# Preparing q, k and v of a block-sorted attention in front of an FFN: batch 0 on 128 partitions and five PSUM banks, v of batches 1 to 3 sorted as the moving operand and scattered through HBM

## The chip, the cores and the metric

One core of a Trainium2 chip runs the whole kernel. The metric is the device time of one execution in microseconds. Unless said otherwise, times inside the execution are counted from the first instruction of the profiled execution (the "span").

## The reference

Inputs: q, k and v of shape (4, 8, 768, 64), `sort_net` (4, 8, 8, 8), FFN weights (512 x 2048 and 2048 x 512) and `alpha` (2048), all fp32. Output: (3072, 512) fp32.

```python
P = sort_net
for _ in range(5):
    P = exp(P - max(P, -1)); P /= sum(P, -1); P /= sum(P, -2)     # eps 1e-9 in each sum
k_sorted = einsum('bhij,bhjcd->bhicd', P, k in 8 blocks of 96)     # the same for v
scores = q_block @ k_sorted_block.T / 8                            # block by block
attn_out = softmax(scores) @ v_sorted_block
x = attn_out.transpose(0, 2, 1, 3).reshape(3072, 512)
h = x @ w_in
out = (max(h, 0) + alpha * min(h, 0)) @ w_out
```

So each (batch, block) pair is an independent attention over 96 rows for 8 heads. There are 32 such pairs; the text calls them groups 0 to 31, eight to a batch.

## The kernel before

**How the order is made.** The kernel adds operations to a graph (`G.add`: engine, function, planned duration, read and write keys, priority). `schedule` (L87) orders them on each engine by planned times and priorities; `emit` (L169) writes five in-order instruction streams with semaphore waits. On the chip nothing is reordered: an instruction that waits holds everything behind it on its engine. DMAs are issued by POOL (loads that cast fp32 to bf16, and so use its software queue) and SP (the small loads, transposes, outputs). `fill` (L152) puts dummy matmuls (L743) into planned gaps of PE up to a time limit.

**Sinkhorn** (L403). P lies as 32 x 64 on DVE; each of five rounds is exponential (ACT, L413), row sum, reciprocal, product, column sum, reciprocal, product (DVE, L415 to L424); round 1 adds eps to the column sums (L421). `spread_k` and `spread_v` (L427, L442) turn P into block matrices BDK and BDV by a small matmul and three DVE operations.

**K of a batch** (`prep_k`, L480): 6 units, each 16 matmuls of 64x64 and one copy of 512 columns from PSUM into KT. **V of a batch**: 8 reshaping copies (`conv_v`, L498, from VST with c and d exchanged into VD), then 8 units (`prep_v`, L510) of 8 matmuls with a slice of VD as the stationary operand and BDV as the moving one, and a copy of each into VS[n]. VS has for each head and block 64 columns and a column of ones, which gives the softmax sums. For batch 0, VST holds 64 partitions; batches 2 and 3 share one set of 8 copies. **Q**: batch 0 by 24 transposing matmuls and 12 copies (`prep_q`, L458) into QTz, in which the other head's 64 rows are zero (two DVE memsets, L373); batches 1 to 3 by loads into QN (zeroed by a POOL memset, L376) and six DMA transposes each on SP (`turn_q`, L345). The next loads of QN wait for the transposes of the batch before.

**Attention of a group** (L531): scores (L544), maxima on DVE (L549), scores again with the maxima subtracted (L557, L562), exponential on ACT (L568), product with VS (the "PV", L576), division by the sums (L581, L584), transposition (L593), copy to xT. **FFN** (L605, L633): FFN1 in chunks of 2, 2 and then 4 groups, 16 row tiles each, through two banks of psH: four matmuls (L613), a Relu on ACT (L621), a DVE operation (L624) into hT. FFN2 is 16 matmuls of 512 columns per 128 tokens (L645), a copy, an output DMA.

**Order of the issue.** POOL: q, k, v of batch 0, w_in in four parts, w_out in two, the memset of QN, k, v and q of batch 1, and the rest as buffers come free. Batch b + 1 is prepared among the groups of batch b. PSUM: psS, psO, psH two banks each, psY and psP one each; the preparation of batch 0 goes through psP and psH.

Of the kernel before, what the change touches and what calls it, by code (L numbers as in the profile page):

```python
# [13 lines left out]
NB = 8  # L14
# [8 lines left out]
XR = 1536  # L23
EPS = 1e-9
# [31 lines left out]
class _Graph:  # L56
# [30 lines left out]
    def schedule(self):  # L87
# [30 lines left out]
        while done < len(ops):  # L118
# [14 lines left out]
            if op.dma is not None:  # L133
                free[e] = at + (600 if e == "pool" else 100)
                begin = max(dma_free if e == "pool" else 0, free[e] + 700)
                if e == "pool":
                    dma_free = begin + dur
                op.end = begin + dur + (1500 if e == "pool" else 500)
            else:
                op.end = free[e] = at + dur  # L140
# [11 lines left out]
    def fill(self, make, unit, first, before):  # L152

        out, last = [], self.ops[first].end + 300
        for op in self.order["pe"]:
            n = int((op.start - last) * 0.9 / unit)
            if op.start < before and n > 0:
# [79 lines left out]
def bass_sinkhorn_attn__then__act_prelu_kernel(  # L237
# [38 lines left out]
    selv = sb("selv", [32, 2, 128], F32)  # L276
# [3 lines left out]
    BDV = sb("BDV", [128, 2, 128], BF16)  # L280
# [4 lines left out]
    xT = sb("xT", [128, KT_TILES, XR], BF16)  # L285
    hT = sb("hT", [128, FT_TILES, RING], BF16)
# [6 lines left out]
    KT = [sb("KT%d" % n, [128, 4, S], BF16) for n in range(2)]  # L293
    VS = [sb("VS%d" % n, [96, 64, 65], BF16) for n in range(2)]
    nm = [sb("nm%d" % n, [96, 8], BF16) for n in range(2)]
    Esb = [sb("Esb%d" % n, [96, 8, 96], BF16) for n in range(2)]
# [8 lines left out]
    psY = ps("psY", [128, 512], F32)  # L305
    psP = ps("psP", [128, 512], F32)
    psPb = psP.bitcast(BF16)
    psOb = psO.bitcast(BF16)
    psHb = psH.bitcast(BF16)
    BANK_P = (psP, psPb, 0, 512, PSP)  # L310
    BANK_H = [(psH, psHb, x * 512, 1024, [("psH", x, 0), ("psH", x, 1)]) for x in range(2)]
# [22 lines left out]
    def load_q(b, prio):  # L334
# [4 lines left out]
        for h in range(H):  # L339
# [3 lines left out]
                load_us / 8, r=["QN0"], w=[("QN", h)], prio=prio, dma=(d_qn[h], 0))  # L343

    def turn_q(b, t, prio):  # L345
# [5 lines left out]
            w=[("QTz", n, u, x, y) for u in range(3) for x in range(2) for y in range(2)] if t == 0 else [("QTzt", n, t)],  # L351
# [6 lines left out]
    def load_v(b, prio):  # L358
        G.add(POOL, lambda e: e.dma_start(
# [5 lines left out]
    def consts():  # L365
# [6 lines left out]
        for hp in range(2):  # L372
            G.add(DVE, lambda e, hp=hp: e.memset(  # L373
                AP(QTz[0], (1 - hp) * 64 * 6144 + hp * 3072, [[6144, 64], [1, 3072]]), 0.0),
                850, w=[("QTz0", 0, hp)], prio=-89)
        G.add(POOL, lambda e: e.memset(QN[:, :, :, :], 0.0), 6000, w=["QN0"], prio=-20)  # L376
        for n in range(2):
            G.add(DVE, lambda e, n=n: e.memset(AP(VS[n], 64, [[64 * 65, 96], [65, 64]]), 1.0), 200,
                  w=[("VS1", n)], prio=-60 + 30 * n)

        def red(o, src, w):
# [6 lines left out]
              r=["identf"], w=["mkj"], prio=-70)  # L388
        red(mvh[:, :], AP(identf, 0, [[128, 128], [8, 16], [1, 8]]), "mvh")
        red(mvj[:, :], AP(identf, 0, [[128, 128], [1, 8], [8, 16]]), "mvj")  # L390
        for t, w, name in ((selk, 16, "selk"), (selv, 8, "selv")):
            G.add(ACT, lambda e, t=t, w=w: copy(e, AP(t, 0, [[32 * w, 32], [w, 32], [1, w]]),
                                                AP(identf, 0, [[128, 32], [1, 32], [0, w]])), 600,
                  r=["identf"], w=[name], prio=-66)
        return ib.idx
# [7 lines left out]
    def sinkhorn():  # L403
# [4 lines left out]
        for it in range(5):  # L408
# [11 lines left out]
            if it == 0:  # L420
                dv(lambda e: e.tensor_scalar(out=cs[:, :], in0=cs[:, :], scalar1=EPS, scalar2=None,  # L421
                                             op0=AluOpType.add), ["cs"], ["cs"])
# [4 lines left out]
    def spread_k(b, prio):  # L427
        G.add(PE, lambda e: e.matmul(psP[:, 0:64], AP(selk, b * 128, [[512, 32], [1, 128]]),
                                     P32[:, :]), 500, r=["P", "selk"], w=PSP, prio=prio)
        G.add(DVE, lambda e: e.tensor_tensor(  # L430
            out=AP(dtmp, 0, [[64, 128], [8, 8], [1, 8]]), in0=AP(psP, 0, [[512, 128], [8, 8], [1, 8]]),
# [10 lines left out]
    def spread_v(hf, prio):  # L442
        G.add(PE, lambda e: e.matmul(psP[:, 0:64], AP(selv, hf * 128, [[256, 32], [1, 128]]), P32[:, :]),
              500, r=["P", "selv"], w=PSP, prio=prio)
        G.add(DVE, lambda e: e.tensor_tensor(
            out=AP(dtmp, 0, [[64, 128], [8, 8], [1, 8]]), in0=AP(psP, 0, [[512, 128], [8, 8], [1, 8]]),
# [5 lines left out]
            out=AP(BDV, hf * 128, [[256, 128], [8, 16], [1, 8]]),  # L452
            in0=AP(mvh, 0, [[16, 128], [1, 16], [0, 8]]),
            in1=AP(dsel, 0, [[8, 128], [0, 16], [1, 8]]), op=AluOpType.mult), 290,
            r=["dsel", "mvh"], w=[("BDV", hf)], prio=prio)


    def prep_q(b, u, prio, bank=BANK_P):  # L458
        n = b % 2
        _, t, off, row, keys = bank  # L460

        def f(e):
            inst = None
            for p in range(8):
                pr = 8 * u + p
                inst = e.matmul(AP(t, 2 * off + p * 128, [[2 * row, 128], [1, 128]]),
                                AP(QS[n], pr * 128, [[3072, 128], [1, 128]]),
                                identb[:, :], is_transpose=True)
            return inst
        G.add(PE, f, t_pe(*[(128, 128)] * 8), r=[("QS", n), "identb"], w=keys, prio=prio)  # L470
        for cp in range(2):
            for hp in range(2):
                o = AP(QTz[n], hp * 64 * 6144 + hp * 3072 + cp + 16 * u,
# [24 lines left out]
    def conv_v(b, u, prio):  # L498
        hf = b // 2
        row, rows, keys = (0, 128, (0, 1)) if b == 2 else ((b % 2) * 64, 64, (b % 2,))  # L500
        if b == 3:
            return
# [161 lines left out]
    for u in range(3):  # L664
        prep_q(0, u, -50, ([BANK_P] + BANK_H)[u])
# [120 lines left out]
```

## Time and profile before

| what | value |
|---|---|
| time, median of 3 runs | 297.44 us (293.62 to 298.7) |
| the profiled execution | 295.86 us, its span 293.9 us |
| mean granted PE clock over the span | 0.936 |
| PE busy | 271.6 us (92%), 2827 matmuls |
| PE weight loads busy | 191.9 us (65%) |
| DVE busy | 189.5 us (64%) |
| ACT busy | 155.2 us (53%) |
| POOL busy | 35.3 us (12%) |
| HBM read / written | 27.28 MB / 6.29 MB |

The busy shares are means over unlike stages. PE's busy time is modelled from pipelined matmuls: it counts a matmul running at half clock, or one with gaps inside its pipeline, as busy too. "Granted clock" is the share of its full rate that the TensorE clock had. In the lines of the timeline, the columns are start, duration, engine, line, operation, output and inputs; a count "x8" merges eight in a row, and brackets give idle time before it and what ended it.

### The profile page before, as it was taken

What the parts mean: (1) busy time and instruction counts of PE and PEld (TensorE: products, weight loads), DVE (VectorE), ACT (ScalarE), POOL (GpSimd) and SP (SyncE); (2) the same over time, 40 slices, a digit from 0 to 9 for tenths busy, and PEclk for the clock granted to TensorE, in tenths of its full rate; (3) what the DMA queues carried; (4) which work ended last, traced back from release to release, by engine and by line L of the source; (5) the groups of instructions that cost most, each with busy time, mean ns of one, the idle gap of its engine ahead of it and who ended that gap; (6) DMA issues with size and microseconds to landing.
All of it is one profiled execution on the core that took longest, in us unless ns stands there. A gap on an engine that the chain in (4) does not pass through costs nothing.

```text
span 293.9 us, 6514 instructions
## 1 busy us (share of the span) xinstructions
PE 271.6 (92%) x2827; PEld 191.9 (65%) x2862; DVE 189.5 (64%) x360; ACT 155.2 (53%) x274; POOL 35.3 (12%) x45
## 2 busy tenths in 40 slices
PE   5909999995997999999999999999999999999995
PEld 5907898883885577776666666766666666655542
DVE  7978356796686578967566766666666666654510
ACT  3079622389689455664545544674454444444421
POOL 8980100001800620000000000000000000000000
PEclk9965555799999999999999999999999999999999
DMA  6999999982999990001671101000101000100111
GB/s 114 214 201 193 213 202 189 182 149 49 195 117 165 148 84 3 4 34 38 153 99 38 38 1 38 36 36 2 38 36 39 36 2 36 38 36 36 38 71 71
DMA packets 46619, 25.07 MB, mean 85 GB/s; under 512 B 38512, under 2 KB 42624, under 8 KB 46336
## 3 DMA queue, kind: packets, MB, share of 16 engines
q0 software_dynamic: 24048, 13.63, 33.6%
q1 hardware_dynamic: 22544, 11.03, 15.4%
q8 instruction: 22, 0.36, 0.5%
q14 instruction: 5, 0.04, 0.0%
HBM read 27.28 MB, written 6.29 MB: 114 GB/s over the span
## 4 chain that ended last, share of the span: by engine, by line
PE 81%; ACT 9%; DVE 7%; issue 2%
PE psH L613 26%; PE psY L645 23%; PE psS L544 4%; PE psS L562 4%; PE psS L557 4%; ACT VD L314 4%; PE psO L576 4%; PE psP L519 4%; PE psS L645 4%; DVE cs L421 2%; PE psY L743 2%; PE psO L593 2%; PE psP L489 2%; ACT t L621 1%; ACT Esb L568 1%
## 5 line engine op out<-in xcount | busy, mean ns | idle before, releaser
L624 DVE SCALAR_TENSOR_TENSOR hT<-t,omaT,psH 128x384 bf16<-128x384 f32 (+1 forms) x144 | 80.2, 566 | 56.5 <-ACT t L621 55.7
L613 PE MATMUL psH<-xT,w_in_bf 128*128 128x384 bf16 (+1 forms) x576 | 101.6, 310 | 4.1 <-DVE hT L624 4.1
L621 ACT ACTIVATE t<-psH 128x384 f32<-128x384 f32 (+1 forms) x144 | 64.2, 454 | 64.2 <-PE psH L613 63.7
L645 PE MATMUL psY<-w_out_bf,hT 128*128 128x512 bf16 x302 | 78.6, 379 | 2.1 <-issue 0.2
L613 PEld LDWEIGHTS psH<-xT,w_in_bf 128*128 128x128 bf16 x576 | 50.3, 99 | 27.8 <-DVE hT L624 5.5
L645 PEld LDWEIGHTS psY<-w_out_bf,hT 128*128 128x128 bf16 x336 | 31.1, 98 | 27.2 <-ACT outstg L314 0.4
L568 ACT ACTIVATE Esb<-psS 96x768 bf16<-96x768 f32 x32 | 25.9, 808 | 27.1 <-PE psS L562 26.6
L549 DVE TENSOR_REDUCE nm<-psS 96x8 bf16<-96x768 f32 x32 | 30.4, 951 | 8.4 <-PE psS L544 7.0
L557 PE MATMUL psS<-QTz,KT 128*96 128x192 bf16 x128 | 27.0, 263 | 0.0
L562 PE MATMUL psS<-identb,nm 96*96 96x96 bf16 x256 | 27.0, 216 | 0.0
L562 PEld LDWEIGHTS psS<-identb,nm 96*96 96x96 bf16 x256 | 25.7, 133 | 1.8
L584 DVE TENSOR_TENSOR xq<-psO,rec 96x512 bf16<-96x512 f32 x32 | 22.0, 686 | 1.1
L340 POOL DMA_DIRECT2D QN<-in_q_dram x24 | 19.9, 885 | 18.7 <-DMA QTz<-QN 18.5
L743 PE MATMUL psY<-identb 128*128 128x128 bf16 x201 | 18.3, 263 | 3.3 <-ACT identb L314 3.3
L314 ACT ACTIVATE VD<-VST 64x768 bf16<-64x768 bf16 (+1 forms) x14 | 21.2, 1525 | 0.1
L576 PEld LDWEIGHTS psO<-VS,Esb 96*96 96x96 bf16 x256 | 16.8, 131 | 5.1 <-ACT Esb L568 0.9
L544 PEld LDWEIGHTS psS<-KT,QTz 128*96 128x96 bf16 x256 | 16.5, 133 | 4.1 <-ACT Esb L568 0.5
L557 PEld LDWEIGHTS psS<-QTz,KT 128*96 128x96 bf16 x128 | 16.9, 132 | 2.8
L544 PE MATMUL psS<-KT,QTz 128*96 128x96 bf16 x256 | 18.3, 218 | 0.4 <-ACT Esb L568 0.4
L743 PEld LDWEIGHTS psY<-identb 128*128 128x128 bf16 x201 | 15.5, 119 | 4.1 <-ACT identb L314 3.3
L576 PE MATMUL psO<-VS,Esb 96*96 96x65 bf16 x256 | 17.4, 214 | 0.3 <-ACT Esb L568 0.2
L314 ACT ACTIVATE outstg<-psY 128x512 f32<-128x512 f32 x21 | 12.6, 599 | 8.2 <-PE psY L645 8.2
(77 smaller groups left out, 220.6 us busy)
## 6 DMA issues: line engine op xcount, KB each, us to landing
out_dram<-outstg SPq DMA_DIRECT2D x24, 256.0 KB, 2.0
KS<-in_k_dram POOLq DMA_DIRECT2D x4, 768.0 KB, 16.6
VST<-in_v_dram POOLq DMA_DIRECT2D x4, 768.0 KB, 19.8
QN<-in_q_dram POOLq DMA_DIRECT2D x24, 96.0 KB, 9.1
w_in_bf<-in_moe_w_in_dram POOLq DMA_DIRECT2D x4, 512.0 KB, 18.9
w_out_bf<-in_moe_w_out_dram POOLq DMA_DIRECT2D x2, 1024.0 KB, 28.3
QS<-in_q_dram POOLq DMA_DIRECT2D x1, 768.0 KB, 7.0
QTz<-QN SPq DMA_TRANSPOSE x18, 3.4
```

The source lines that it names most:

```text
L314: return e.activation(o, i, ACTF.Copy) if e is nc.scalar else e.tensor_copy(o, i)
L544: inst = e.matmul(AP(psS, (s // 4) * 512 + (s % 4) * 96, [[1024, 96], [1, 96]]), AP(QTz[n], hp * 3072 + h4 * 768 + i * 96, [[6144, 128], [ ...
L549: G.add(DVE, lambda e: e.tensor_reduce(AP(nm[m], 0, [[8, 96], [4, 2], [1, 4]]), AP(psS, 0, [[1024, 96], [512, 2], [96, 4], [1, 96]]), Axis ...
L557: e.matmul(AP(psS, base, [[1024, 96], [1, 192]]), AP(KT[n], h4 * 768 + i * 96, [[3072, 128], [1, 96]]), AP(QTz[n], h4 * 768 + i * 96, [[61 ...
L562: inst = e.matmul(AP(psS, base + hp * 96, [[1024, 96], [1, 96]]), AP(nm[m], 2 * h4 + hp, [[8, 96], [0, 96]]), AP(identb, 0, [[128, 96], [1 ...
L568: G.add(ACT, lambda e: e.activation(AP(Esb[m], 0, [[768, 96], [384, 2], [1, 384]]), AP(psS, 0, [[1024, 96], [512, 2], [1, 384]]), ACTF.Exp ...
L576: inst = e.matmul(AP(psO, hp * 512 + h4 * 68, [[1024, 96], [1, 65]]), AP(Esb[m], s * 96, [[768, 96], [1, 96]]), AP(VS[n], ((hp * 4 + h4) * ...
L613: inst = e.matmul(AP(psH, hb * 512, [[1024, 128], [1, n]]), AP(w_in_bf, kt * DFF + ft * 128, [[KT_TILES * DFF, 128], [1, 128]]), AP(xT, kt ...
L621: G.add(ACT, lambda e: e.activation(AP(t1[tb], 0, [[384, 128], [1, n]]), AP(psH, hb * 512, [[1024, 128], [1, n]]), ACTF.Relu, scale=-1.0), ...
L624: G.add(DVE, lambda e: e.scalar_tensor_tensor(out=AP(hT, ft * RING + tok % RING, [[FT_TILES * RING, 128], [1, n]]), in0=AP(t1[tb], 0, [[38 ...
L645: inst = e.matmul(AP(bank[0], bank[1], [[row, 128], [1, 512]]), AP(hT, ft * RING + tok % RING, [[FT_TILES * RING, 128], [1, 128]]), AP(w_o ...
L743: inst = e.matmul(psY[:, 0:128], identb[:, :], identb[:, :])
```

## The change

In words:

- L421's addition of a constant becomes an addition of two tensors, with a small tile of eps. The two memsets of QTz go. POOL's memset of QN is cut into eight, which fill only the halves that no load writes. A new POOL memset zeroes 16 pad columns of VD.
- Batch 0: v is loaded onto 128 partitions (two halves of each block), first of the three; q is loaded last. `conv_v` is four copies; `prep_v` 8 units of 16 matmuls of 64x64; the 96 rows of a block stand as 48 + 16 (zero) + 48 in the 112 rows of VS[0]. K gets 16 columns of padding by a copy (`KTpad`). The column of ones becomes a DVE copy from a tile `one0`, which is 0 in the pad rows. `prep_q` works like `prep_k` with the identity, without zero rows; scores of batch 0 are matmuls over 64 rows of one head. The 20 units of k, v and q go through five banks. Groups 0 and 1 use different banks for scores and outputs.
- Batches 1 to 3: v is sorted by matmuls with BDV as the stationary operand and VST as the moving one (512 columns, 12 per batch; batches 2 and 3 in the same 12 steps), copied to VD, written to an HBM tensor, and read back into VS in pieces of 64 elements. Each batch has two halves; all these DMAs go through SP's queue.
- The spreads of batches 1 to 3 are bound behind group 1. The planner's constants for POOL's DMAs (1500 to 2500 ns) and the dummy matmuls' limits change.

The core of the diff:

```diff
-        for hp in range(2):
-            G.add(DVE, lambda e, hp=hp: e.memset(
-                AP(QTz[0], (1 - hp) * 64 * 6144 + hp * 3072, [[6144, 64], [1, 3072]]), 0.0),
-                850, w=[("QTz0", 0, hp)], prio=-89)
-        G.add(POOL, lambda e: e.memset(QN[:, :, :, :], 0.0), 6000, w=["QN0"], prio=-20)
+        G.add(DVE, lambda e: e.memset(epst[:, :], EPS), 100, w=["eps"], prio=-89)
+        G.add(POOL, lambda e: e.memset(AP(VD, 48, [[6144, 128], [64, 64], [1, 16]]), 0.0), 900,
+              w=["VD0"], prio=-95.5)
+        for h in range(H):
+            G.add(POOL, lambda e, h=h: e.memset(
+                AP(QN, h * 128 + (1 - h // 4) * 64, [[6144, 128], [1024, 6], [1, 64]]), 0.0),
+                400, w=[("QN0", h)], prio=-21)
...
+        G.add(DVE, lambda e: e.tensor_copy(AP(VS[0], 64, [[64 * 65, 112], [65, 64]]), AP(one0, 0, [[1, 112], [0, 64]])),
+              200, r=["one0"], w=[("VS1", 0)], prio=-70)
...
-                dv(lambda e: e.tensor_scalar(out=cs[:, :], in0=cs[:, :], scalar1=EPS, scalar2=None,
-                                             op0=AluOpType.add), ["cs"], ["cs"])
+                dv(lambda e: e.tensor_tensor(out=cs[:, :], in0=cs[:, :], in1=epst[:, :], op=AluOpType.add),
+                   ["cs", "eps"], ["cs"])
...
     def load_v(b, prio):
+        if b == 0:
+            G.add(POOL, lambda e: e.dma_start(
+                AP(VST, 0, [[6144, 128], [1, 3072]]),
+                AP(v.tensor, 0, [[3072, 2], [6144, 64], [1, 3072]])),
+                load_us, w=[("VST", 0), ("VST", 1)], prio=prio, dma=(d_v[0], 0))
+            return
...
+    def prep_q(u, prio, bank):
+        t, off, row, keys = bank
+        G.add(PE, pairs(QS[0], 0, u, identb, 0, 128, bank), 8 * 33, r=[("QS", 0), "identb"], w=keys, prio=prio)
+        o = AP(QTz[0], 8 * u, [[6144, 128], [96, 32], [48, 2], [1, 8]])
+        i = AP(t, off, [[row, 128], [2, 32], [1, 2], [64, 8]])
+        G.add(EITHER, lambda e: copy(e, o, i), t_either(512), r=keys, w=[("Q0", u)], prio=prio)
...
+        if b == 0 and u == 1:
+            G.add(DVE, lambda e: e.tensor_copy(AP(KT[0], 48, [[ld, 128], [bk, 32], [1, 16]]),
+                                               AP(KT[0], 0, [[ld, 128], [bk, 32], [1, 16]])), 500,
+                  r=[("KT", 0, 0), ("KT", 0, 1)], w=["KTpad"], prio=prio + 1)
+
+    def conv_v(u, prio):
+        o = AP(VD, 16 * u * 64, [[6144, 128], [64, 16], [1, 48]])
+        i = AP(VST, 16 * u, [[6144, 128], [1, 16], [64, 48]])
+        G.add(EITHER if u == 3 else ACT, lambda e: copy(e, o, i), {"act": 1520, "dve": 890},
+              r=[("VST", 0), ("VST", 1)] + ["P"] * (u == 3), w=[("VD", u)], prio=prio)
...
+    def sort_v(bs, c, prio):
+        row, rows, keys = (bs[0] % 2) * 64, 64 * len(bs), [("VST", b % 2) for b in bs]
+
+        def f(e):
+            inst = None
+            for b in bs:
+                r0 = (b % 2) * 64
+                inst = e.matmul(AP(psYP, r0 * 1024 + 512, [[1024, 64], [1, 512]]),
+                                AP(BDV, r0 * 384 + (b // 2) * 128 + r0, [[384, 64], [1, 64]]),
+                                AP(VST, r0 * 6144 + c * 512, [[6144, 64], [1, 512]]))
+            return inst
+        G.add(PE, f, 300, r=keys + [("BDV", b // 2) for b in bs], w=PSP, prio=prio)
+        G.add(EITHER, lambda e: copy(e, AP(VD, row * 6144 + c * 512, [[6144, rows], [1, 512]]),
+                                     AP(psYP, row * 1024 + 512, [[1024, rows], [1, 512]])), t_either(512), r=PSP,
+              w=[("VN", c, b % 2) for b in bs] + ([("VD", u) for u in range(4)] + ["VD0"] if c == 0 else []), prio=prio)
+
+    def turn_v(b, x, prio):
+        r0, n = (b % 2) * 64, b % 2
+        G.add(SYNC, lambda e: e.dma_start(AP(scr, b * 64 * 6144 + x * 3072, [[6144, 64], [1, 3072]]),
+                                          AP(VD, r0 * 6144 + x * 3072, [[6144, 64], [1, 3072]])),
+              4000, r=[("VN", c, b % 2) for c in range(6 * x, 6 * x + 6)], w=[("scr", b, x)], prio=prio,
+              dma=(d_vo[2 * b + x], 0))
...
+        G.add(SYNC, lambda e: e.dma_start(AP(VS[n], x * 48 * 64 * 65, [[64 * 65, 48], [65, 64], [1, 64]]),
+                                          AP(scr, b * 64 * 6144 + x * 3072, [[64, 48], [6144, 64], [1, 64]])),
+              9000, r=[("scr", b, x), ("VS1", n)],
+              w=[("VS", n)] + [("VSu", u) for u in range(8)] * (n == 0) if x == 0 else [("VSx", n)],
+              prio=prio, dma=(d_vi[2 * b + x], 0))
...
-    load_q(0, -98)
+    load_v(0, -98)
     load_k(0, -97)
-    load_v(0, -96)
+    load_q(0, -96)
...
+    for u in range(4):
+        conv_v(u, -50)
+    bank = 0
+    spread_k(0, -48)
+    spread_v(2, -47.5)
+    for name, count, prio in (("k", 6, -47), ("v", 8, -45), ("q", 6, -46)):
+        for u in range(count):
+            x = BANKS0[bank % 5]
+            bank += 1
+            prep_k(0, u, prio, x) if name == "k" else prep_v(u, prio, x) if name == "v" else prep_q(u, prio, x)
...
-            units = ([(prep_k, u) for u in range(6)]
-                     + [(conv_v, u) for u in range(8)] + [(prep_v, u) for u in range(8)])
+            vs = ([1],) if b == 0 else ([2, 3],) if b == 1 else ()
+            if b == 2 and i == 0:
+                for x in range(2):
+                    turn_v(3, x, 8 * b - 7)
+            units = ([(f, x, c) for x in vs for y in range(2) for f, c in
+                      [(sort_v, c) for c in range(6 * y, 6 * y + 6)] + [(None, y)]]
+                     + [(prep_k, b + 1, u) for u in range(6)])
```

## The prediction

> **What bounds the kernel now.** I read the stage table first (the busy time of each engine in chosen stretches), then the timeline of the start, then the waits of PE, then the DMA queues. Columns of the stage table: stretch, its length, busy us and count of PE, PEld, DVE, ACT, POOL, granted clock, DMA share, GB/s.
>
> ```profile
> 0.00:24.00 24.00, 13.33 (x182) 13.04 (x183) 19.86 (x47) 10.69 (x19) 19.89 (x25) 0.87 0.99 179
> 24.00:50.00 26.00, 25.77 (x296) 22.59 (x295) 14.89 (x33) 13.02 (x16) 1.10 (x2) 0.50 1.40 196
> 50.00:74.00 24.00, 19.91 (x283) 16.09 (x285) 18.12 (x38) 17.11 (x30) 1.99 (x4) 0.89 0.77 135
> 74.00:98.00 24.00, 21.50 (x291) 17.11 (x294) 17.20 (x36) 19.38 (x35) 5.73 (x7) 1.00 1.19 165
> 98.00:146.00 48.00, 47.61 (x543) 33.83 (x549) 35.35 (x61) 26.84 (x50) 6.56 (x8) 1.00 0.40 57
> ```
>
> From 98 us on PE has no gap: only less PE work or an earlier start can move the end. Before 98 us PE is late or half idle, and from 24 to 50 us it runs at clock 0.50. The timeline says why the start is late:
>
> ```profile
> 6.12 7.32 DVE L421 TENSOR_SCALAR cs<-cs 32x8 f32<-32x8 f32 x1
> 8.13 5.29 POOL L376 MEMSET QN<- 128x6144 bf16 x1
> 13.71 0.26 DVE L424 TENSOR_TENSOR P<-P,cs 32x64 f32<-32x64 f32 x1
> 21.98 0.69 PE L428 MATMUL psP<-P,selk 32*128 32x64 f32 x2 [7.32 <-DVE P L424]
> 52.61 1.47 PE L613 MATMUL psH<-xT,w_in_bf 128*128 128x192 bf16 x8
> 95.04 0.51 PE L576 MATMUL psO<-VS,Esb 96*96 96x65 bf16 x8
> ```
>
> An addition to 256 numbers takes 7.32 us and ends at 13.44, as POOL's memset ends (13.42): DVE was held by POOL. P is ready at 21.9, the first FFN matmul runs at 52.6, and the ninth PV product (L576, group 8, the first of batch 1) at 95.0. From there to the end are 293.9 - 95.0 = 198.9 us, nearly all PE work. Last, the DMA side, which the change will load:
>
> ```profile
> 50.20 13.64 SPq L347 DMA_TRANSPOSE QTz<-QN  x6
> 75.02 0.38 SPq L655 DMA_DIRECT2D out_dram<-outstg  x1
> 87.73 8.61 SPq L347 DMA_TRANSPOSE QTz<-QN  x6
> ```
> ```profile
> 98.25 6.56 POOL L340 DMA_DIRECT2D QN<-in_q_dram  x8 [18.52 <-DMA QTz<-QN]
> ```
> ```profile
> DMA packets 6367, 1.35 MB, mean 168 GB/s; under 512 B 6288, under 2 KB 6288, under 8 KB 6355
> ```
>
> The first fence is SP's queue: batch 1's transposes start when q has landed, at 50.2, and hold SP for 13.6 us; batch 2's hold it for 8.6. The second is POOL: a batch of q takes 6.6 us to issue, and only after the transposes of the batch before. The third is the DMA page of 42 to 50 us, when batch 1's q arrives: 6288 small packets in 8 us, 786 per us. Until then the queue carries weights and inputs at some 200 GB/s, and the change alters neither their bytes nor, but for the order inside them, their place: q of batch 1 still lands near 50.2.
>
> **The change, part by part.** The sum is made on the profiled execution (span 293.9, time 295.86, so 2 us lie around the span); it is 1.6 us below the median of 297.44.
>
> Sinkhorn. L421 becomes a two-operand addition; its neighbour L417 takes 0.21, so -7.1. The two memsets of QTz (1.34 each) go, and the first exponential can start after selk (3.8) instead of 4.84: -1.0. P would be ready at 13.8. But the new ones column of VS (line 402 of the changed kernel, a DVE copy from SBUF to SBUF) stands between rounds 1 and 2 of the chain, at about 6 us, when POOL is again busy: issues till about 9 (before: 8.1, plus about 0.9 for the new memset of VD, 1024 elements at 0.86 ns), then eight memsets of QN, half the elements in all. It may cost nothing, or hold DVE until POOL's memsets end near 13, as L421 was. I take a release between two of the eight memsets, near 9.5: P at 9.5 + 4 rounds of 1.87 = 17; ends 13.8 and 21.
>
> The rule that speaks against this step is in the Trainium skill, "SBUF — State Buffer", Who interferes with whom: a DVE copy in a two-port mode and a GpSimd instruction exclude each other for the whole instruction, and the later one waits. L421 (7.32 us) agrees. By the rule alone, with POOL's eight memsets taken as one occupation, the copy would wait to about 13 and P come at 21; with the copy free, at 13.8; the end would be the same, as the sum below shows.
>
> Preparation of batch 0. Q no longer goes through 12 copies of 0.75 on ACT/DVE but through 6 units like K; V keeps 8 units, its 8 reshaping copies (1.5 on ACT, 0.9 on DVE) become 4. 20 units follow BDK (P + 2.5, as now 21.9 to 24.3): on PE each is 16 matmuls, 0.56 from start to start at clock 0.50 (27.86 to 28.43), 11.2 in all; their 20 copies of 0.6 to 0.69 on two engines and five banks take 6.6 beside it. First scores at 17 + 2.5 + 11.5 = 31. Then L544 twice (0.7 each), L549 0.95, the score matmuls twice (1.3), exponential 0.81, L576, L581 and L584 0.9, L593, copy 0.49, with hand-overs some 9.5 for two groups: first FFN at 40.5 instead of 52.6.
>
> To group 8. From first FFN to the PV of group 8 the old kernel takes 42.4 us (PE idle 6.6 of it, by the waits mostly on DVE and ACT behind the 1.5 us copies L314). The built order of the new one has 16 more FFN1 matmuls of 384 columns (0.65 per 4: +2.6), 16 more FFN2 (0.86 per 4: +3.4), 18 v-sort matmuls (0.22 each by L645, some in pairs: +3.6), 8 old V units fewer (0.39 from start to start: -3.1), two K units fewer (0.37 each: -0.7), two score units and a PV more (+1.1), four spreads (0.5 each, between 0.69 at half clock and half of it: +2): about +9, against up to 6.6 of idle that ends with the ACT copies. So 45 to 51, taken as 46: PE could reach that PV at 40.5 + 46 = 86.5, against 95.0.
>
> VS through HBM. That PV now waits for two DMAs per batch in SP's queue, and the built order of SP is: six transposes of batch 1, an output, V out (half 0), V in (half 0), V out (half 1), **six transposes of batch 2**, V in (half 1). So the second half, which PE needs, queues behind transposes that wait for q of batch 2, and these loads wait for the transposes of batch 1. The chain: 50.2 + 13.6 = 63.8 on SP; landed by 66 (landing median 3.4); eight q loads 6.6 on POOL and a landing of 4.4 in the quiet stretch: 76.5; six transposes 8.0 to 8.6, some more beside the load of V of batch 3: 86; V in, 3072 pieces of 128 B at 786 per us = 3.9, and 2.0 as an output DMA takes: 92. The trace has no such DMA; from below 2.0 + 2.7 (transposes move faster), from above the 13.6 us that the crowded transposes took: 90.5 to 99.5. I take 92, since the q pieces are of the same size and number per us. The wait stands on PE's queue, so all FFN work behind it waits too; ACT and DVE drain. PE also waits in front of the first v-sort of batches 2 and 3 for V of batch 3, which POOL issues after the q loads: 73 + 9.2 (least landing of VST) = 82, inside the same wait.
>
> A page gives another price: the Trainium skill, "DMA: Bandwidth & Descriptors", Anatomy of one DMA, fits a software-queue DMA by 2.0 us + bytes / 436 GB/s, which makes an estimate of 2.9 us for these 393 KB and would put the PV at 89. The same page, Specifications, asks for at least 512 B per piece for full rate, and the row of 786 small pieces per us (about 100 GB/s at 128 B) agrees.
>
> After that PV the built order holds less PE work: 16 FFN1 matmuls (-2.6), 16 FFN2 (-3.4), 16 V units (-6.2), one score unit (-0.4); more: 18 v-sort matmuls, in pairs on different halves of the array (+2.0 to +3.9), two K units (+0.7). About -9: 198.9 - 9 = 190. Fewer ACT copies there win nothing, PE being full. A gap of 5 us or more before it lets the clock fall as it did after 14.7 us (0.89 at 16 to 18, then 0.50): half speed for about 3 us costs 1.5.
>
> Sum: 92 + 190 + 1.5 = 283.5 span, + 2 = **285.5**, that is -10 against the profiled run. Gains in the start beyond this are lost in the wait; a held copy at line 402 (up to +4, 90.5 at PE) costs nothing as long as the wait ends at 92, and its whole excess if DVE is held past about 13.
>
> **Rivals.** (a) No wait at group 8: if batch 1's transposes take 8.6 instead of 13.6, everything in the chain comes 5 us earlier (87) and PE's own 86.5 decides: 87 + 190 + 2 = 279; with P at 13.8, 276. For: the second and third sets took 8.0 to 8.6. Against: q and V of batch 2 are still loading behind q of batch 1, as now. (b) The wait is longer: transposes of batch 2 at 13.6 and V in at 8 to 10: 76.5 + 13.6 + 10 = 100, so 100 + 190 + 1.5 + 2 = 293.5, within 2%. For: they share the DMA engines with V of batch 3. (c) Slower: V in is far costlier than q pieces. One place, SP's last entry before the PV. To be slower by 2% (303.4) the PV must come at 110, 24 us after its issue, six times the rate of the q pieces; at 30 us the time is 309.5. Against: nothing in the trace moves 128 B pieces that slowly. (d) The fix does not fix: DVE is held for the whole of POOL's work to about 18; P at 25.5, PE at the PV at 95, 95 + 190 + 2 = 287, still faster since the work after it is less.
>
> **How the numbers follow.** Forecast (PV at 90 to 95, with or without d) 0.5, a 0.2, b 0.2, c 0.1 (0.08 of it slower, the rest within 2%). The time is the forecast's, 285.5; its own range is 283 to 289. The range to 294 takes in b, from 276 a; c is left out with what lies below 276. About 2% is what this measurement can tell from no change: faster means under 291.5. Faster: forecast, a and 0.03 of b, 0.73; within 2%: the other 0.17 of b and 0.02 of c, 0.19; slower: 0.08.
>
> **What would show it.** L421's successor at 0.2; P between 13.8 and 21; first FFN near 40; SP's last V entry of batch 1 behind batch 2's transposes, and PE's longest wait after 50 us at the PV of group 8, for the DMA of VS, ending near 92; from there 190 us without gaps. Wrong if PE has no wait there (a), if the copy at line 402 takes over 10 us, if V in lands more than 12 us after issue (b, c), or if PE shows new gaps after 100 us.

## The result, and the profile after

The changed kernel takes 324.24 us (median of 4 runs, 322.16 to 324.93) against 297.31 for the kernel before in the same measurement: ratio 1.0945, 95% interval 1.0846 to 1.1043. The forecast was 285.5. The profiled execution has a span of 320.4 us. One remark on all times below: the kernel before took about 297.6 us in most executions and 291 to 294 in a few, and before_eps about 291 in seven of ten and 299 to 302 in three, so ratios leave out what is over 1.5% above the kernel's shortest, and times without a ratio are medians of all executions, beside 297.6 to 298.0 for the kernel before.

The stage table of the changed kernel, in the stretches shown for the kernel before:

```profile
0.00:24.00 24.00, 11.59 (x170) 11.41 (x170) 6.07 (x30) 3.27 (x8) 16.17 (x29) 0.87 0.97 164
24.00:50.00 26.00, 7.89 (x196) 7.01 (x197) 7.95 (x25) 8.19 (x11) 4.16 (x6) 0.57 1.34 187
50.00:74.00 24.00, 20.81 (x330) 17.26 (x327) 11.65 (x27) 7.82 (x14) 0.00 (x0) 0.64 0.43 66
74.00:98.00 24.00, 22.88 (x214) 14.86 (x219) 16.01 (x39) 13.16 (x31) 6.58 (x8) 0.89 1.09 114
98.00:146.00 48.00, 41.19 (x456) 26.73 (x460) 25.33 (x48) 27.55 (x56) 7.69 (x10) 0.93 1.29 150
```

From 24 to 50 us PE is busy 7.9 us where it was busy 25.8, and DVE 8.0 and ACT 8.2: each stands idle for two thirds of the stretch, while the DMA moves 187 GB/s, much as before (196). The timeline says who waits:

```profile
5.29 0.15 DVE L439 TENSOR_TENSOR cs<-cs,epst 32x8 f32<-32x8 f32 x1
5.88 0.41 DVE L402 CAST VS<-one 112x64 bf16<-112x64 f32 x1
9.33 0.26 DVE L442 TENSOR_TENSOR P<-P,cs 32x64 f32<-32x64 f32 x1
33.80 1.50 ACT L318 ACTIVATE VD<-VST 128x768 bf16<-128x768 bf16 x1 [25.74 <-DMA VST<-in_v_dram]
35.48 0.21 DVE L433 TENSOR_REDUCE rs<-P 32x8 f32<-32x64 f32 x1 [25.89 <-ACT P L431]
38.84 0.68 PE L447 MATMUL psYP<-P,selk 32*128 32x64 f32 x2 [23.61 <-DVE P L442]
39.91 0.55 POOL L369 DMA_DIRECT2D VST<-in_v_dram  x1 [22.15 <-DVE dtmp L449]
68.69 1.07 PE L679 MATMUL psH<-xT,w_in_bf 128*128 128x192 bf16 x8
75.57 13.12 SPq L351 DMA_TRANSPOSE QTz<-QN  x6
107.60 12.61 SPq L351 DMA_TRANSPOSE QTz<-QN  x6
120.26 0.58 SPq L563 DMA_DIRECT2D VS<-v_sorted_dram  x1
127.25 0.85 PE L640 MATMUL psO<-VS,Esb 96*96 96x65 bf16 x8 [5.44 <-DMA VS<-v_sorted_dram]
```

Three rounds of Sinkhorn run without a stop and end at 9.6. The exponential of round 4 then stands on ACT behind the first reshaping copy of v, which waits 25.7 us for the load of v; P is ready at 38.8. POOL's next load of v, which overwrites what the copies read, is issued at 39.9, after them, and the rest of batch 1's q behind it: batch 1's transposes start at 75.57 (before: 50.20). The first FFN matmul comes at 68.7 (52.6), the PV of group 8 at 127.25 (95.04). The columns of the DMA page are the transfer, the issuing queue, count, size and the median time from issue to landing, over all batches where the count is 4; first the load that stood first in the kernel before (its other medians: KS 16.6, VST 19.8, w_in 18.9), then the changed kernel:

```profile
QS<-in_q_dram POOLq DMA_DIRECT2D x1, 768.0 KB, 7.0
```

```profile
VST<-in_v_dram POOLq DMA_DIRECT2D x4, 768.0 KB, 33.1
KS<-in_k_dram POOLq DMA_DIRECT2D x4, 768.0 KB, 36.5
QS<-in_q_dram POOLq DMA_DIRECT2D x1, 768.0 KB, 37.9
w_in_bf<-in_moe_w_in_dram POOLq DMA_DIRECT2D x4, 512.0 KB, 42.1
VS<-v_sorted_dram SPq DMA_DIRECT2D x6, 384.0 KB, 10.1
```

The first load of all, v of batch 0, takes 32.5 us (by itself; 33.1 is the median of four) where q in that place took 7.0. K and q behind it take 35.2 and 37.9, where k and v behind q took 9.9 and 14.8 before, although the total rate is nearly the old one. In the account of the time: the PV of group 8 is 32.2 us later, what follows it is 5.7 us shorter (193.2 against 198.9), together the 26.5 us of the spans.

Theory T: the source of this load is written as `[[3072, 2], [6144, 64], [1, 3072]]`, its outermost step has two values, and only two DMA engines carry it. Of its 128 pieces (6144 B each), the trace's records of single transfers show just two in flight at 15, 18, 22, 26 and 30 us, where the kernel before has 16 to 18 between 4 and 10 us; a piece takes 0.474 us in the median, and 64 x 0.474 = 30.3. That the two in flight are two engines is inferred: the records name no engine. The Trainium skill, "DMA: Bandwidth & Descriptors", Why a DMA increments its semaphore by 16 and not by 1, has this rule: the number of engines is the largest up to 16 that divides the slowest dimension of both patterns, here 2. The prediction did not weigh it. There are three rivals. R: a load of 128 partitions, or the first place in the queue, is slow. H: only the order on ACT is at fault. S: the way through HBM is the loss.

### The profile page after: what moved, and what is told of

Read it like the earlier page. It is cut to its first block, busy times and chain, and to the rows that moved or that the text cites. A ratio compares the mean times of both kernels' runs of the same rounds, so it can differ in the third digit from the quotient of the medians.

```text
span 320.4 us, 6603 instructions
## 1 busy us (share of the span) xinstructions
PE 274.1 (86%) x2871; PEld 182.7 (57%) x2904; DVE 170.9 (53%) x349; ACT 139.3 (43%) x265; POOL 34.6 (11%) x53
## 3 DMA queue, kind: packets, MB, share of 16 engines
q0 software_dynamic: 25008, 13.64, 32.2%
## 4 chain that ended last, share of the span: by engine, by line
PE 77%; DMA 12%; SPq 3%; issue 3%; DVE 2%; ACT 1%; POOLq 0%
PE psH L679 26%; PE psYP L711 21%; DMA VST<-in_v_dram 10%; PE psS L604 4%; PE psO L640 4%; SPq L351 3%; PE psS L711 3%; PE psS L591 3%; PE psS L612 3%; PE psYP L485 2%; PE psYP L545 2%; DMA VS<-v_sorted_dram 2%; PE psYP L820 2%; PE psO L659 2%; PE psS L622 1%
## 5 line engine op out<-in xcount | busy, mean ns | idle before, releaser
L711 PE MATMUL psYP<-w_out_bf,hT 128*128 128x512 bf16 x304 | 80.1, 382 | 2.4 <-issue 1.0
L679 PEld LDWEIGHTS psH<-xT,w_in_bf 128*128 128x128 bf16 x576 | 50.8, 100 | 26.5 <-issue 1.8
L711 PEld LDWEIGHTS psYP<-w_out_bf,hT 128*128 128x128 bf16 x336 | 30.9, 98 | 27.8 <-issue 1.2
L632 ACT ACTIVATE Esb<-psS 96x768 bf16<-96x768 f32 (+1 forms) x31 | 25.0, 807 | 33.8 <-PE psS L604 33.4
L344 POOL DMA_DIRECT2D QN<-in_q_dram x24 | 19.8, 857 | 62.5 <-DMA QTz<-QN 62.5
L604 PE MATMUL psS<-identb,nm 96*96 96x96 bf16 (+1 forms) x248 | 23.7, 214 | 0.0
L604 PEld LDWEIGHTS psS<-identb,nm 96*96 96x96 bf16 (+1 forms) x248 | 21.7, 129 | 2.0
L447 PE MATMUL psYP<-P,selk 32*128 32x64 f32 x8 | 2.5, 406 | 23.6 <-DVE P L442 23.6
L820 PE MATMUL psYP<-identb 128*128 128x128 bf16 x229 | 19.1, 256 | 3.6 <-ACT identb L318 3.6
L640 PEld LDWEIGHTS psO<-VS,Esb 96*96 96x96 bf16 (+1 forms) x248 | 15.9, 129 | 11.0 <-DMA VS<-v_sorted_dram 5.7
L640 PE MATMUL psO<-VS,Esb 96*96 96x65 bf16 (+1 forms) x248 | 16.7, 213 | 5.9 <-DMA VS<-v_sorted_dram 5.4
L820 PEld LDWEIGHTS psYP<-identb 128*128 128x128 bf16 x229 | 16.9, 116 | 4.1 <-ACT identb L318 3.6
L318 ACT ACTIVATE outstg<-psYP 128x512 f32<-128x512 f32 x21 | 12.5, 597 | 8.8 <-PE psYP L711 8.8
L318 ACT ACTIVATE VD<-VST 128x768 bf16<-128x768 bf16 x3 | 4.5, 1490 | 25.7 <-DMA VST<-in_v_dram 25.7
## 6 DMA issues: line engine op xcount, KB each, us to landing
VST<-in_v_dram POOLq DMA_DIRECT2D x4, 768.0 KB, 33.1
w_out_bf<-in_moe_w_out_dram POOLq DMA_DIRECT2D x2, 1024.0 KB, 52.6
```

Of the source, the lines that this page charges most:

```text
L344: G.add(POOL, lambda e, h=h: e.dma_start(AP(QN, h * 128 + (h // 4) * 64, [[6144, 128], [1024, 6], [1, 64]]), AP(q.tensor, b * HB + h * S * ...
L604: return e.matmul(AP(psX, (p // 4) * 512 + (p % 4) * 96, [[1024, nk], [1, 96]]), AP(nm[m], p, [[8, 96], [0, nk]]), AP(identb, 0, [[128, 96 ...
L632: G.add(ACT, lambda e: e.activation(AP(Esb[m], 0, [[768, nk], [384, 2], [1, 384]]), AP(psX, 0, [[1024, nk], [512, 2], [1, 384]]), ACTF.Exp ...
L640: inst = e.matmul(AP(psZ, hp * 512 + h4 * 68, [[1024, 96], [1, 65]]), AP(Esb[m], pos(h4, hp) * 96, [[768, nk], [1, 96]]), AP(VS[n], ((hp * ...
L679: inst = e.matmul(AP(psH, hb * 512, [[1024, 128], [1, n]]), AP(w_in_bf, kt * DFF + ft * 128, [[KT_TILES * DFF, 128], [1, 128]]), AP(xT, kt ...
L711: inst = e.matmul(AP(bank[0], bank[1], [[row, 128], [1, 512]]), AP(hT, ft * RING + tok % RING, [[FT_TILES * RING, 128], [1, 128]]), AP(w_o ...
```

## The experiments

**v0_halves.** Two loads of 64 partitions under one semaphore; every engine's order is otherwise that of the changed kernel.

```diff
-    e.dma_start(AP(VST, 0, [[6144, 128], [1, 3072]]), AP(v.tensor, 0, [[3072, 2], [6144, 64], [1, 3072]]))
+    for th in range(2):
+        e.dma_start(AP(VST, th * 64 * 6144, [[6144, 64], [1, 3072]]), AP(v.tensor, th * 3072, [[6144, 64], [1, 3072]]))
```

> The changed kernel with the load of v of batch 0 split in two loads of 64 partitions each; bytes, pieces, targets and the order of every engine stay. Theory T (the load's rows are taken in an order whose outermost step has only two values, so only two DMA engines carry it: 128 pieces of 6144 B at the trace's median of 0.474 us a piece are 64 x 0.474 = 30.3 us on two engines, and it landed 33.1 us after its issue): spread over sixteen engines it is 8 x 0.474 = 3.8 us, so it lands 7 to 9 us after its issue, P is ready at 13 to 17 instead of 38.8, batch 1's transposes start near 50 instead of 75.6, the PV of group 8 runs at 92 to 103, and with the 192 us that follow it in the changed kernel and 2 around the span the time is 286 to 297. Rival R (128 partitions, or being first in POOL's queue, makes it slow): it lands over 20 us after its issue and the time stays over 312. Rival S (the way of v through HBM for batches 1 to 3 is the loss): P comes early as in T, but the PV of group 8 stays near 128 and the time over 310.

Measured: 300.03 us (299.25 to 302.49; before 297.96). From the DMA page, then the timeline:

```profile
VST<-in_v_dram POOLq DMA_DIRECT2D x2, 384.0 KB, 5.6
QS<-in_q_dram POOLq DMA_DIRECT2D x1, 768.0 KB, 13.2
```
```profile
13.18 0.26 DVE L448 TENSOR_TENSOR P<-P,cs 32x64 f32<-32x64 f32 x1
16.19 0.43 PE L453 MATMUL psYP<-P,selk 32*128 32x64 f32 x2
41.58 1.46 PE L685 MATMUL psH<-xT,w_in_bf 128*128 128x192 bf16 x8
82.09 15.36 SPq L351 DMA_TRANSPOSE QTz<-QN  x6
97.50 0.58 SPq L569 DMA_DIRECT2D VS<-v_sorted_dram  x1
104.66 0.85 PE L646 MATMUL psO<-VS,Esb 96*96 96x65 bf16 x8 [9.36 <-DMA VS<-v_sorted_dram]
```

T holds: the two halves land 4.9 and 6.2 us after their issues (5.6 in the median), P is ready at 13.4, the first FFN matmul runs at 41.6, 24 of the 27 us come back. The time is 3 us above T's range, and PE now waits 9.4 us, from 95.3, for the second half of VS, which SP issues only after batch 2's transposes. S falls as the main cause, with a rest that stays, and so does the first place in the queue; a load of 64 partitions does not yet rule out that 128 are slow, which before_q2 decides.

**conv_late.** The slow load stays, the copies wait for P.

```diff
-              r=[("VST", 0), ("VST", 1)] + ["P"] * (u == 3), w=[("VD", u)], prio=prio)
+              r=[("VST", 0), ("VST", 1), "P"], w=[("VD", u)], prio=prio)
```

> The changed kernel, slow load and all, but the first three reshaping copies of v on ACT (line 318 by conv_v) are made to wait for P as the fourth does, so that ACT's exponentials no longer stand behind a copy that waits for the load. Rival H (the standing of the exponentials behind that copy is the whole loss): P at 13 to 15 and a time of 285 to 297. Theory T (the load itself and the loads that share its two engines are late): P at 13 to 15 as well, but K of batch 0 still lands after 36 and v after 33, so the first FFN matmul comes at 55 or later, POOL's next load of v still waits for the copies, and the time is 310 to 322.

Measured: 327.91 us (327.46 to 330.48). PE's longest waits:

```profile
PE psYP L462 <- DVE dtmp L449: 19.3, 1, 19.3
PE psO L640 <- DMA VS<-v_sorted_dram: 12.3, 1, 12.3
```

The first spread runs at 14.6, and the next product stands on DVE behind that engine's own copy of v: the block has moved from ACT to DVE. K of batch 0 lands too late for it to matter (PE waits 2.0 us more for KS). H falls: without the block PE could not have begun K before 37.5 either. The time is above even T's range; what goes with it is the wait of 12.3 us, as the planner now puts the second write of v as well behind batch 2's transposes in SP's queue, and other work on PE, ACT and DVE elsewhere.

**before_q2, before_q4.** The kernel before, the rows of its first load (q of batch 0) taken in another order; q's rows of batch 0 are thereby permuted.

```diff
-    AP(q.tensor, 0, [[3072, 128], [1, 3072]])
+    AP(q.tensor, 0, [[3072, 2], [6144, 64], [1, 3072]])         # before_q2
+    AP(q.tensor, 0, [[3072, 4], [4 * 3072, 32], [1, 3072]])     # before_q4
```

> The kernel before with one change: q of batch 0, its first load, is read with its rows in the order that the changed kernel uses for v (outermost step of two values), into the same 128 partitions; the rows of q of batch 0 are thereby permuted, so that part of the output is another function of the input. Theory T: q lands 30 us or more after its issue instead of 7.0, the k, v and w_in loads behind it land 10 us or more later than before (16.6, 19.8, 18.9), and the time rises by 10 to 30 us, to 307 to 327. Rival R (it is v, its place, or what the changed kernel does with it): q lands near 7 and the time stays within 2 us of before.

> The kernel before with q of batch 0 read with its rows in an order whose outermost step has four values (row a + 4 t into partition 32 a + t), into the same 128 partitions, same 128 pieces of 6144 B; as in before_q2 this permutes the rows of q of batch 0. Theory T (the outermost count of the rows sets how many DMA engines carry the load): 32 pieces x 0.474 us = 15.2 us an engine, so q lands 16 to 20 us after its issue, between 7.0 (128 rows in order) and 32.6 (outermost two), and the time stands between those of before and before_q2 (315.4), at 298 to 308. Rival O (any order that jumps over rows makes it slow): it lands near 32 as in before_q2. Rival N (only the count two is bad): near 7.

Measured: 315.42 us (315.25 to 317.1) and 307.56 (305.68 to 307.86; ratio 1.0316, interval 1.0259 to 1.0374). The landing of q in before_q2, then in before_q4:

```profile
QS<-in_q_dram POOLq DMA_DIRECT2D x1, 768.0 KB, 32.6
```
```profile
QS<-in_q_dram POOLq DMA_DIRECT2D x1, 768.0 KB, 23.6
```

7.0, 23.6, 32.6 us for outermost counts 128, 4, 2: the same disease in a kernel without any of the change and with the same order on every engine, with mostly 2 (before_q2) and mostly 4 (before_q4) of these pieces in flight from 15 us on. All three loads go into 128 partitions, so R falls. Rival O falls too: with four the load lands at 23.6 and not near 32, and the two loads of v0_halves, which also jump over rows, land in 4.9 and 6.2. With four engines it lands later than the 16 to 20 expected: between 14 and 20 us its pieces take 0.69 instead of 0.474; why is open, since in before_q2, with the same loads behind it, they took 0.474. T's mechanism is shown; its arithmetic holds only for two.

**before_eps, before_eps2.** The kernel before with nothing but the two-operand addition at L421.

```diff
-    e.tensor_scalar(out=cs[:, :], in0=cs[:, :], scalar1=EPS, scalar2=None, op0=AluOpType.add)
+    e.tensor_tensor(out=cs[:, :], in0=cs[:, :], in1=epst[:, :], op=AluOpType.add)
```

> The kernel before with only the addition of line 421 made a two-operand addition. By the prediction's step (7.1 us off the start of P): P ready at 14 to 15 instead of 21.9. If the start decides the end, the time falls by 4 to 8 us, to 289 to 293. If the next stage (k of batch 0 landing at 16.6, v at 19.8, batch 1's transposes at 50.2) takes it back, the time falls by less than 3 us.

> before_eps once more, beside v0_halves_sp on one chip, for a profile of a typical execution. If its gain is the earlier P (16.0 instead of 21.9 at the first spread): first FFN matmul at 46 to 48, PV of group 8 at 88 to 91, time 289 to 293. If the gain is something else, the PV of group 8 stays at 95.

Measured: 291.68 us (290.12 to 302.39) and 295.37 (289.57 to 299.68); ratio of the second to before 0.9764 (0.9697 to 0.9832). With this scatter the size of the gain is not settled. The timeline of before_eps2, whose profiled execution took 289.57:

```profile
15.84 0.43 PE L430 MATMUL psP<-P,selk 32*128 32x64 f32 x2 [1.01 <-DVE P L426]
46.48 1.47 PE L615 MATMUL psH<-xT,w_in_bf 128*128 128x192 bf16 x8
88.76 0.51 PE L578 MATMUL psO<-VS,Esb 96*96 96x65 bf16 x8
```

A spread that starts 6.1 us earlier moves the first FFN matmul by 6.1, the PV of group 8 by 6.3 and the span by 6.3 (287.6 against 293.9): in this pair the start decides the end. The profile of before_eps (302.39 us, span 300.4) shows that an early start alone does not. From its timeline, then from PE's waits:

```profile
16.05 0.43 PE L430 MATMUL psP<-P,selk 32*128 32x64 f32 x2 [1.01 <-DVE P L426]
```
```profile
PE psP L521 <- ACT VS L315: 12.3, 1, 12.3
```

The start is as early, but a load of v issued at 66.5 lands 23.2 us later (10.8 in before_eps2); ACT waits 12.1 us for it, PE 12.3 for ACT, and the PV of group 8 comes at 101.57. What held that load is open.

**v0_halves_sp, v0_halves_sp2.** After planning, one entry of SP is moved up.

```diff
+    sp, x, y = G.order["sync"], vin[1, 1], tq[2, 0]     # VS load of batch 1, half 1; first transpose of batch 2
+    sp.remove(x)
+    sp.insert(sp.index(y), x)
```

> The kernel v0_halves with one entry of SP's queue moved: batch 1's second VS load now stands ahead of batch 2's six transposes instead of behind them (it was issued at 97.5 there, and PE waited from 95.3 to 104.7 for it). Theory Q (place in the queue): it is issued near 84, lands by 96 at the 10.6 us of the other VS loads, PE's wait at the PV of group 8 goes from 9.4 us to under 2, and with 193 us behind that PV and 2 around the span the time is 288 to 292. Rival C (the transfers themselves, crowded): moved up, it collides with q of batch 2 and the transposes, lands 15 us or more after its issue, and the time stays over 296.

> v0_halves_sp once more, beside before_eps on one chip. 294 to 295.5 again if its time is steady; if before_eps is at 289 to 293, the addition of line 421 alone is worth more than the whole change with both of its faults mended.

Measured: 294.71 us (294.38 to 295.09) and 294.69 (290.85 to 295.38); ratio of the second to before 0.9861 (0.9781 to 0.9941). So with both faults mended the change is at most a little faster than the kernel before: 1.4% is under the 2% that the prediction took as what can be told from no change. Against before_eps (0.9764) the intervals overlap, so which of the two is faster is open. The timeline of v0_halves_sp, then a row of its stage table (columns as before):

```profile
78.32 1.04 SPq L564 DMA_DIRECT2D v_sorted_dram<-VD  x1
91.16 0.32 SPq L571 DMA_DIRECT2D VS<-v_sorted_dram  x1
91.79 11.13 SPq L353 DMA_TRANSPOSE QTz<-QN  x6
98.21 0.85 PE L648 MATMUL psO<-VS,Esb 96*96 96x65 bf16 x8 [2.89 <-DMA VS<-v_sorted_dram]
```
```profile
100.00:104.00 4.00, 4.00 (x26) 2.49 (x24) 0.71 (x3) 2.17 (x4) 0.00 (x0) 0.50 1.43 187
```

The wait shrinks from 9.4 to 2.9 us (Q), but the load is issued at 91.2, not 84: the write to HBM in front of it takes 12.8 us, until then. The time lies between the two theories. In v0_halves_sp2 PE waited 3.8 us for the load of v of batch 3 instead, in front of the same PV.

**v0_noread.** v0_halves, attention of batches 1 to 3 reading batch 0's sorted v; all of the traffic stays, into a buffer that nobody reads. The planner then also orders some work on PE, ACT, DVE and SP differently.

```diff
-    AP(VS[n], ((hp * 4 + h4) * 8 + i) * 65, [[64 * 65, nk], [1, 65]])
+    AP(VS[0], ((hp * 4 + h4) * 8 + i) * 65, [[64 * 65, nk], [1, 65]])
```

> The kernel v0_halves where attention of batches 1 to 3 reads batch 0's sorted v (so their output is another function of v), while v of these batches is still sorted, written to HBM and read back as before, into a buffer that nobody reads. This takes PE's waits for the way through HBM away and keeps its DMA traffic and its PE work. Theory Q: PE has no wait at group 8 and the time is 288 to 292, like v0_halves_sp. If the waits cost more than the one at group 8, it is below 287; if the extra PE work and traffic are the rest of the loss and not the wait, it stays over 296.

Measured: 290.77 us (289.27 to 291.66), as Q expects: 9.3 below v0_halves, about the wait of 9.4. The PV of group 8:

```profile
95.95 0.51 PE L643 MATMUL psO<-VS,Esb 96*96 96x65 bf16 x8
```

So PE itself comes to that PV near 96, where v0_halves has it idle from 95.3. What the traffic costs by itself no run shows, as none leaves it out and keeps the rest.

**vs_contig.** v0_halves_sp, the same bytes, but each partition of a VS load is one piece of 8 KB (the order of v is scrambled).

```diff
-    e.dma_start(AP(VS[n], x * 48 * 64 * 65, [[64 * 65, 48], [65, 64], [1, 64]]),
-                AP(scr, b * 64 * 6144 + x * 3072, [[64, 48], [6144, 64], [1, 64]]))
+    e.dma_start(AP(VS[n], x * 48 * 64 * 65, [[64 * 65, 48], [1, 4096]]),
+                AP(scr, b * 64 * 6144 + x * 48 * 4096, [[4096, 48], [1, 4096]]))
```

> The kernel v0_halves_sp with the same bytes written to HBM and read back into VS, but laid down so that each of the 48 partitions of a VS load is one piece of 8 KB instead of 64 pieces of 128 B; the order of v is thereby scrambled and most of the column of ones overwritten, so the output of batches 1 to 3 is another function of v. Theory P (the 128 B pieces make the load long: 3072 of them were costed at 3.9 + 2.0 us and took 10.7 to landing): the VS loads land in 3 to 6 us, PE's wait of 2.9 us at the PV of group 8 goes to under 0.5, and the time falls by 1 to 4 us, to 291 to 293.5. Rival C (the crowd on the DMA engines makes it long): they still land in 8 us or more and the time stays within 1 us of 294.7.

Measured: 287.75 us (287.4 to 288.44), ratio 0.9674 (0.9635 to 0.9712). Its DMA page:

```profile
VS<-v_sorted_dram SPq DMA_DIRECT2D x6, 384.0 KB, 4.7
```

The load takes 4.7 instead of 10.7 to 11.9 in the two runs of v0_halves_sp, PE no longer waits for it, and the time falls by 7, more than the 1 to 4 expected. Against v0_halves_sp the PV of group 8 is at 94.6, 3.6 us earlier, and 191.6 us follow it instead of 194.6; PE's clock, which there falls to 0.50 after the wait (the row of 100 to 104 us above), stays at 1.00. (In v0_halves_sp2 the lost time lies in front of the PV: it is at 101.1, and 191.6 follow.) Every engine's order is the same in both kernels, so piece size (P) is shown. It helps the transfers beside it as well: the second write to HBM, in 6 KB pieces in both, takes 7.8 instead of 12.8 us, and the load of v of batch 3, issued beside it, 7.7 instead of 13.0.

**scatter_write.** Could the small pieces go to the other transfer? v0_halves_sp with v and its ones in VD, written in 130 B pieces and read back whole; what is computed stays.

```diff
+    e.dma_start(AP(scr, base, [[65, 64], [4160, 48], [1, 65]]), AP(VD, r0 * 6240 + x * 48 * 65, [[6240, 64], [65, 48], [1, 65]]))
+    e.dma_start(AP(VS[n], x * 48 * 4160, [[4160, 48], [1, 4160]]), AP(scr, base, [[4160, 48], [1, 4160]]))
```

> The kernel v0_halves_sp with the small pieces on the other transfer: v sorted stands in VD with its column of ones (65 elements a token), is written to HBM in 3072 pieces of 130 B already in the order of VS, and read back with one piece of 8.3 KB for each partition. What is computed stays. Theory P (a transfer of small pieces takes its 10 us whichever way it goes): the write lands in 9 to 13 us instead of 6.7 to 8.8, the read in 4 to 6 instead of 10.7 to 11.9, the two together in 14 to 18 as now, and the time is 292 to 296. Rival W (small pieces cost less on the way to HBM): the write lands in under 8 us, PE has no wait over 1 us at the PV of group 8, and the time is 286 to 290, below both kernels.

Measured: 317.22 us (315.1 to 319.35), ratio 1.0642 (1.0565 to 1.0719).

```profile
v_sorted_dram<-VD SPq DMA_DIRECT2D x6, 390.0 KB, 19.7
VS<-v_sorted_dram SPq DMA_DIRECT2D x6, 390.0 KB, 5.5
```

Both theories miss: written in small pieces nearly the same bytes take 19.7 us, about twice as long as read in small pieces. PE waits 8.9 us in front of group 8 for the load of v of batch 3, and 17.1 in front of group 16, whose last VS load lands at 171.4, 0.1 us before its PV.

**b0_only.** v0_halves with v of batches 1 to 3 prepared as in the kernel before.

```diff
-    units = [sort_v ..., turn_v ...] + [(prep_k, b + 1, u) for u in range(6)]
+    units = [(prep_k, u) for u in range(6)] + [(conv_v1, u) for u in range(8)] + [(prep_v1, u) for u in range(8)]
```

> The kernel v0_halves with the new preparation of batch 0, and with v of batches 1 to 3 prepared as in the kernel before (reshaping copies, eight units of eight matmuls, no way through HBM). It prices the two parts of the change. If the new batch 0 is the gain (first FFN matmul at 41.6 instead of 52.6) and the way through HBM neither gains nor loses once its wait is gone: PV of group 8 at 84 to 92 and, with the 199 us that follow it in the kernel before, a time of 285 to 293. If the sorting through HBM saves the 9 us of PE work behind group 8 that the prediction counted, b0_only is 3 to 8 us slower than v0_halves_sp; if it saves nothing, b0_only is as fast or faster.

Measured: 303.14 us (302.92 to 304.08), 8.4 above v0_halves_sp, just over the 3 to 8 expected. 201.3 us follow its PV of group 8 (at 100.3), against 194.6 (191.6 in the second run); PE is busy for 196.4 of them against 189.6 (186.7): sorting as the moving operand saves about 7 to 10 us of PE time there. In front of it the windows show why it is not at 84 to 92 (columns as in the stage table):

```profile
60.00:64.00 4.00, 2.48 (x47) 1.68 (x46) 3.45 (x6) 3.96 (x6) 1.05 (x1) 1.00 1.00 69
64.00:68.00 4.00, 2.58 (x28) 1.85 (x25) 1.70 (x5) 3.97 (x6) 0.00 (x0) 0.60 1.33 220
68.00:72.00 4.00, 3.35 (x19) 2.39 (x21) 1.92 (x5) 1.84 (x5) 0.00 (x0) 0.50 1.08 170
```

ACT is full with the 1.5 us copies of v, PE is busy 5.1 of 8 us, and its clock falls to 0.50 for the next 20 us. That the clock fell because of the pause is only the order of the rows, and the kernel before speaks against a simple rule:

```profile
64.00:68.00 4.00, 3.24 (x57) 2.17 (x55) 2.57 (x6) 3.97 (x6) 0.00 (x0) 1.00 0.29 64
68.00:72.00 4.00, 2.20 (x36) 1.60 (x36) 3.33 (x6) 3.94 (x6) 0.57 (x1) 1.00 0.12 15
```

There PE is busy 5.4 of 8 us, also beside a full ACT, and the clock stays at 1.00.

## Why the prediction was wrong, point by point

**L421.** Right: 0.15 us, and the pair of before and before_eps2 prices it at 6.3 us, with the scatter said there. The feared hold of the new copy at line 402 did not come (0.41 us while POOL was issuing loads); with the load mended P was ready at 13.4, the early end of the given 13.8 to 21. The first spread then stood at 16.2, behind 170 dummy matmuls on PE.

**The step that failed:** "the change alters neither their bytes nor, but for the order inside them, their place: q of batch 1 still lands near 50.2". The order inside one load was the matter. It put the load of v on two engines (32.5 us to landing, where the first load had taken 7.0), and by the engines' and the queues' order K, q, the weights, P, POOL's loads and batch 1's transposes (75.6) behind it. Neither the sum nor any rival had a term for it; before_q2 and v0_halves show it in both directions: 18 us in, 24 us out.

**Start of the FFN.** 40.5 was forecast, 41.6 is measured once the load is mended. That is in part luck, as the parts miss both ways: the units begin at 17.6 instead of 19.5, take 13.5 us with a pause of 3.1 in them instead of 11.5, the first scores come at 32.7 instead of 31, and 8.9 us follow instead of 9.5.

**To group 8.** 46 us were taken from a range of 45 to 51; v0_halves needs 53.7 (41.6 to 95.3). The idle that was to disappear did not pay for the added work, and the clock was 0.50 from 40 to 52 us in v0_halves_sp. In the kernel before it was back at 1.00 from 56 us on (0.61 from 52 to 56), within 4 us of the first FFN matmul, so the 42.4 us that the sum started from held little of it; some 9 us more at half clock would be 4 to 5 us of work, an estimate from these rows. PE's own arrival was thus 95 (95.95 in v0_noread), not 86.5.

**VS through HBM.** The place was right, the second half stood behind batch 2's transposes and PE's wait was there; the sizes were not. In v0_halves batch 2's transposes start at 82.1 instead of 76.5, as the last of q lands about 9 us after its issue and not 4.4; they hold SP for 15.4 us where the sum had 9.5; and the read takes 7.1 instead of 5.9: 104.6 instead of 92. (The chain's 66 + 6.6 + 4.4 is 77.0, not 76.5.) The chain also had no term for the write in front of the second read: it takes 12.7 us, until 91.3, hidden there behind the transposes, and in v0_halves_sp it is what sets the read. The read that PE waited for was one of the shorter ones: the median of the six is 10.6, and 4.7 with large pieces (vs_contig). So the row taken for the price, 786 small pieces per us of q, was not met, and the skill's estimate of 2.9 us was farther off.

**Behind group 8.** 190 and 1.5 for the clock were forecast, 191.5 together; 193.2 (after) to 193.5 (v0_halves) are measured, against 198.9. In vs_contig, where the clock stays at 1.00, it is 191.6: the work saved is 7 us, not 9. With 104.7 and 193.5 one has 298.2, the span of v0_halves.

Open: the matmuls of the new V units on PE pause 3 us inside one run ("issue", 3.3 in the changed kernel, 3.1 in v0_halves), which no wait in the profile explains; and why the second writes and the transposes take as long as they do.

## What to carry to other kernels

Read a load's access pattern before its byte count: here the outermost count decided how many engines carried it (128, 4 and 2 gave 7.0, 23.6 and 32.6 us), so a reordering that costs nothing on paper may multiply the landing time, and all loads behind it pay. When an in-order engine serves a long chain, keep copies that wait for a DMA out from between its links, or the slowest load sets the chain. A detour through HBM is not priced by its bytes alone: here piece size and place in the issuing queue moved the time at the same bytes.

## What the runs showed of the hardware that was not expected

Reading 393 KB from HBM into SBUF took 10.7 and 11.9 us (medians of the two runs of v0_halves_sp) in 128 B pieces and 4.7 in 8 KB pieces (vs_contig); writing 399 KB to HBM took 19.7 in 130 B pieces (14.2 to 27.1) against 8.8 and 6.7 for 393 KB in 6 KB pieces in the two runs of v0_halves_sp. A load on two engines hardly lowered the total rate (187 GB/s from 24 to 50 us, 196 before): beside its two pieces in flight there were 15 to 19 of 1 KB from later loads, which fits that these filled the other engines and that each finished only with its last share, behind v on the two. The Trainium skill, "DMA: Bandwidth & Descriptors", Specifications, says that pieces under 512 B are read, modified and written; scatter_write agrees in direction, and no run here shows that mechanism.
